# Block 0 of a recurrence with a feed-forward layer: one written order of instructions and loads for all sixteen steps

## The chip, the cores and the metric

The kernel runs on one core of one Trainium2 chip. A core has five engines with a queue of instructions each: PE (TensorE, matmuls), DVE (VectorE), ACT (ScalarE), POOL (GpSimd) and SP (SyncE, which issues the loads here). Each works through its own queue in order and waits at semaphores for the others. The metric is the device time of one execution in microseconds (us), as the median of several runs.

## The reference, cut to what matters

```python
# r, k, v: [B=4, H=8, S=768, D=48], w, u: [H, D], all float32
state = zeros(B, H, D, D)
for t in range(S):
    cur = (u * k[t]) outer v[t]
    y[t] = r[t] @ (state + cur)
    state = w * state + k[t] outer v[t]
x = y as [B * S = 3072, H * D = 384]
h = x @ w_in                          # w_in: [384, 2048]
g = where(h > 0, h, exp(min(h, 0)) - 1)
out = g @ w_out                       # w_out: [2048, 384]
```

## The kernel before, in words

The 768 positions are cut into 6 chunks of 128. A unit (n, b) is one batch b in chunk n, and a block is the four units of a chunk, 512 token columns. In a unit r and k are turned by PE (`turn_in`, L628), scaled by powers of w (`decay_r`, `decay_k`, through `scaled`, L688), multiplied to scores inside the chunk (`scores`, L768), masked or taken over by copies (`mask_scores` at the start, `take_scores`, L849, later), and multiplied by v; the state of the chunk before is added (`by_state`, `by_keys`, `added_state`). A token's own term, r times u times k, is made by `key_product` and `times_u` (L724, L728), summed by `current_sum` (L733) and either put on the scores' diagonal (`diag_scores`, L838 on ACT, L842 on POOL) or, in block 0, multiplied by v (`current_by_v`, L859). `key_rest` (L740) multiplies k by the power of w that is left to the end of the chunk, which the new state needs. `split_x` (L949; `split_turned`, L899 and L901, in block 0) gives the outputs as a high and a low part.

The feed-forward layer of a block goes in 16 steps f of 128 hidden columns: `hidden` (L1031: nine matmuls, since x and the weights stand as high and low parts), `negative` (L1040 and L1041 on ACT: relu and exp), `elu` (L1046 on DVE), `split_g` (L1052 the high part on ACT, L1054 the low one on DVE) and `project` (L1083, nine matmuls that gather in PSUM). The hidden steps have two buffers in PSUM, so step f needs the buffer that the low part of an earlier g gave back.

The weights are loaded within block 0, in stages of one w_out and one w_in slice: `load_weights(j)` is w_in of step j/2 for even j (four DMAs, L212), w_out for odd j (L215). Three stages are held at a time. Pair k (w_out of step k-1, w_in of step k) is brought to its high and low parts by `widen` (ACT, L571), `merge` (DVE, L580), `split_w` (w_out's on POOL, L591; w_in's on ACT, L593) and `rest_w` (w_out's on POOL, L615, or DVE; w_in's on DVE, L617).

The order on every engine follows from the order in which the program calls these functions. Before, three strings set it for block 0: START (written out, to the first half of hidden step 0), BOTH (written out, steps 0 to 2) and FIRST, a pattern that `step` goes through once for each of the steps 3 to 15 and in which an entry with a digit or x means "the unit that is at this stage now" (a unit of block 1 begins at the steps of BEGIN). LATER is the pattern of blocks 1 to 5. The short names are the keys of the tables of operations: `wd`, `ma`, `sp`, `rs` (or `rsd`, on DVE) for the weights, `T`, `dr`, `dk`, `A`, `ru`, `sum`, `kr` (`krd` on DVE) for a unit, `Lw:j` for a load of weights, `Lrk`, `Lv`, `Lnk`, `Lnv`, `rk`, `v` for loads of r and k or v.

Of the kernel before, what the change touches and what calls it, by code (L numbers as in the profile page):

```python
# [8 lines left out]
F32 = mybir.dt.float32  # L9
# [10 lines left out]
P = 128  # L20
# [7 lines left out]
T = B * P  # L28
# [8 lines left out]
EARLY = (0, 6)  # L37
# [22 lines left out]
BEGIN = [2, 5, 8, 11]  # L60
# [6 lines left out]
class Kernel:  # L67
# [232 lines left out]
    def run(self):  # L300
        self.start()
        self.first_steps()
        for at in range(3, NCH * NF):
            self.step(*divmod(at, NF))
        for f in (NF - 2, NF - 1):
            self.project(NCH - 1, f)
        self.store(NCH - 1)

    def start(self):
# [3 lines left out]
        for b in (2, 3):  # L313
# [33 lines left out]
            "m1a": lambda b: self.mask_scores(0, b, 1, True),  # L347
            "vd": lambda b: self.current_by_v(0, b),
# [34 lines left out]
    def first_steps(self):  # L383
# [44 lines left out]
    def step(self, n, f):  # L428
        nc = self.nc

        k = f + 2 if n == 0 else NF + 1
        units = self.stages(n, f)


        last = divmod(n * NF + f - (1 if (n, f) < EARLY else 2), NF)
        both = {
            "ru": lambda n, b: self.current(n, b),
            "kr": lambda n, b: self.key_rest(n, b),
            "A": lambda n, b: self.scores(n, b),
            "sw": lambda n, b: self.decay_state(n, b),  # L440
# [725 lines left out]
```

## Time and profile before

| | |
|---|---|
| median of 3 runs | 497.28 us (496.21 to 499.79) |
| profiled execution, its own time | 496.31 us |
| its span in the profile | 494.6 us |
| mean granted clock of PE | 0.999 |
| PE matmul | 485.3 us busy, 98% of the span |
| PE weight loads (beside the matmuls) | 403.4 us, 82% |
| DVE | 304.2 us, 61% |
| ACT | 240.7 us, 49% |
| POOL | 107.3 us, 22% |

Busy times are sums over the whole span, so a share is a mean over stages that differ. The profile also cuts the span in 40 slices of 12.4 us and gives the busy share of each in tenths; its lines of PE and DVE are

```profile
PE   8999999999999999999999999999999999999995
DVE  7899988884686557657556575574674343433332
```

Block 0 is the first nine slices.

### The profile page before, as it was taken

What the parts mean: (1) busy time and instruction counts of PE and PEld (TensorE: products, weight loads), DVE (VectorE), ACT (ScalarE), POOL (GpSimd) and SP (SyncE); (2) the same over time, 40 slices, a digit from 0 to 9 for tenths busy, and PEclk for the clock granted to TensorE, in tenths of its full rate; (3) what the DMA queues carried; (4) which work ended last, traced back from release to release, by engine and by line L of the source; (5) the groups of instructions that cost most, each with busy time, mean ns of one, the idle gap of its engine ahead of it and who ended that gap; (6) DMA issues with size and microseconds to landing.
All of it is one profiled execution on the core that took longest, in us unless ns stands there. A gap on an engine that the chain in (4) does not pass through costs nothing.

```text
span 494.6 us, 12125 instructions
## 1 busy us (share of the span) xinstructions
PE 485.3 (98%) x5013; PEld 403.4 (82%) x5013; DVE 304.2 (61%) x533; ACT 240.7 (49%) x458; POOL 107.3 (22%) x142
## 2 busy tenths in 40 slices
PE   8999999999999999999999999999999999999995
PEld 7787778787888888888888888888888888889995
DVE  7899988884686557657556575574674343433332
ACT  4377766734454444535435435445354453344341
POOL 7623332441132331221321321301011000000000
PEclk9999999999999999999999999999999999999999
DMA  9899987483364652544513625514343000010001
GB/s 142 223 231 204 213 197 190 94 153 89 84 139 105 135 121 43 130 118 72 121 52 84 151 67 108 142 44 92 101 79 100 11 1 2 8 33 20 5 0 69
DMA packets 108453, 49.11 MB, mean 99 GB/s; under 512 B 89442, under 2 KB 104292, under 8 KB 108388
## 3 DMA queue, kind: packets, MB, share of 16 engines
q1 hardware_dynamic: 96292, 43.52, 40.0%
q10 hardware_dynamic: 12096, 4.72, 4.0%
q8 instruction: 41, 0.67, 0.6%
q14 instruction: 24, 0.20, 0.1%
HBM read 35.12 MB, written 13.11 MB: 98 GB/s over the span
## 4 chain that ended last, share of the span: by engine, by line
PE 93%; DMA 3%; SPq 2%; DVE 1%; issue 0%; ACT 0%; DVEq 0%
PE ps_acc L1083 40%; PE ps_h L1031 39%; PE ps_y L824 4%; PE ps_a L792 4%; PE ps_y L812 1%; PE ps_y L924 1%; PE ps_a L768 1%; PE ps_y L807 1%; DMA raw<-in_k_dram 1%; DMA stage<-in_moe_w_out_dram 1%; DMA r_t<-in_r_dram 1%; SPq L169 1%; PE ps_y L880 1%; SPq L165 1%; PE ps_kT L628 0%; DMA w_col<-in_w_dram 0%
## 5 line engine op out<-in xcount | busy, mean ns | idle before, releaser
L1031 PE MATMUL ps_h<-x,wh 128*128 128x512 f32 (+1 forms) x582 | 192.6, 388 | 0.0
L1083 PE MATMUL ps_acc<-g,wh 128*128 128x512 f32 x480 | 164.6, 397 | 0.1
L1046 DVE SCALAR_TENSOR_TENSOR ps_h<-g,ps_h 128x512 f32<-128x512 f32 x96 | 66.6, 694 | 123.8 <-ACT g L1041 123.6
L1031 PEld LDWEIGHTS ps_h<-x,wh 128*128 128x128 f32 x582 | 108.8, 188 | 23.0 <-DVE g L1054 0.5
L1040 ACT ACTIVATE g<-ps_h 128x512 f32<-128x512 f32 x96 | 57.3, 596 | 123.2 <-PE ps_h L1031 95.0
L1031 PE MATMUL ps_h<-x,wl 128*128 128x512 f32 (+1 forms) x291 | 112.7, 387 | 0.0
L1083 PEld LDWEIGHTS ps_acc<-g,wh 128*128 128x128 f32 x480 | 90.0, 188 | 21.2 <-issue 0.8
L1054 DVE SCALAR_TENSOR_TENSOR g<-ps_h,g 128x512 fp32r<-128x512 f32 x96 | 66.3, 690 | 45.3 <-ACT g L1052 40.4
L1083 PE MATMUL ps_acc<-g,wl 128*128 128x512 f32 x240 | 93.6, 390 | 0.0
L1052 ACT ACTIVATE g<-ps_h 128x512 fp32r<-128x512 f32 x96 | 57.4, 598 | 72.7 <-DVE ps_h L1046 62.7
L1031 PEld LDWEIGHTS ps_h<-x,wl 128*128 128x128 f32 x291 | 54.7, 188 | 10.9
L1041 ACT ACTIVATE g<-g 128x512 f32<-128x512 f32 x96 | 60.7, 632 | 3.1
L842 POOL TENSOR_TENSOR a<-ident,diag 128x512 f32<-128x512 f32 x20 | 20.9, 1044 | 149.9 <-PE ps_y L924 81.2
L1083 PEld LDWEIGHTS ps_acc<-g,wl 128*128 128x128 f32 x240 | 45.1, 188 | 8.5
L676 POOL TENSOR_TENSOR tb<-rk,qw 128x512 f32<-128x512 f32 x16 | 20.7, 1297 | 70.3 <-DMA rk<-blocks 61.2
L1083 PE MATMUL ps_acc<-wh,g 128*128 128x384 f32 x128 | 33.8, 335 | 0.0
L849 DVE COPY_PREDICATED a<-mask,ps_a 128x512 f32<-128x512 int32 x40 | 29.3, 732 | 0.0
L838 ACT ACTIVATE a<-ident,diag 128x128 f32<-128x128 f32 x80 | 25.3, 391 | 0.0
L1083 PEld LDWEIGHTS ps_acc<-wh,g 128*128 128x128 f32 x128 | 23.2, 188 | 0.3
L571 ACT ACTIVATE wide<-stage 128x768 f16<-128x768 bf16 (+1 forms) x18 | 17.8, 991 | 9.9 <-DMA stage<-in_moe_w_in_dram 8.7
L949 ACT CAST x<-ps_y 128x256 fp32r<-128x256 f32 (+1 forms) x40 | 10.8, 324 | 22.8 <-DVE state L939 21.4
L1083 PE MATMUL ps_acc<-wl,g 128*128 128x384 f32 x64 | 21.4, 335 | 0.0
(114 smaller groups left out, 440.2 us busy)
## 6 DMA issues: line engine op xcount, KB each, us to landing
blocks<-tb SPq DMA_DIRECT2D x64, 128.0 KB, 2.3
rk<-blocks SPq DMA_DIRECT2D x16, 512.0 KB, 3.4
stage<-in_moe_w_out_dram SPq DMA_DIRECT2D x16, 383.8 KB, 5.4
stage<-in_moe_w_in_dram SPq DMA_DIRECT2D x64, 95.8 KB, 4.3
out_dram<-stage ACTq DMA_DIRECT2D x80, 48.0 KB, 1.7
r_t<-in_r_dram SPq DMA_DIRECT2D x17, 192.0 KB, 4.3
k_t<-in_k_dram SPq DMA_DIRECT2D x17, 192.0 KB, 4.9
v_t<-in_v_dram SPq DMA_DIRECT2D x17, 192.0 KB, 5.3
```

The source lines that it names most:

```text
L676: (self.nc.gpsimd if i else self.nc.vector).tensor_mul(dst, src, by)
L792: nc.tensor.matmul(un["pa"][i][keys, a * P : (a + 1) * P], lhsT=un["k"][rows, a, keys], rhs=un["r"][rows, a, :], start=True, stop=True, sk ...
L838: self.nc.scalar.activation(un["a"][i][:, a, :], self.ident, AF.Copy, scale=diag[:, a : a + 1])
L842: self.nc.gpsimd.tensor_mul(un["a"][i], self.ident.unsqueeze(1).to_broadcast([P, HP, P]), diag.unsqueeze(2).to_broadcast([P, HP, P]),)
L849: self.nc.vector.copy_predicated(un["a"][i], self.mask.bitcast(I32).unsqueeze(1).to_broadcast([P, HP, P]), un["pa"][i].rearrange("p (a t) ...
L1031: self.nc.tensor.matmul(ph[:, part], lhsT=a[:, c * P : (c + 1) * P], rhs=x[:, c, part], start=(c == 0 and i == 0), stop=(c == NC - 1 and i ...
L1040: nc.scalar.activation(g, ph, AF.Relu, scale=-1.0)
L1041: nc.scalar.activation(g, g, AF.Exp, scale=-1.0)
L1046: self.nc.vector.scalar_tensor_tensor(ph, g, -1.0, ph, op0=ALU.add, op1=ALU.max)
L1052: nc.scalar.activation(part, g, AF.Copy, scale=W_SCALE)
L1054: nc.vector.scalar_tensor_tensor(part, g, W_SCALE, self.g[n, f][2].bitcast(F32), op0=ALU.mult, op1=ALU.subtract)
L1083: self.nc.tensor.matmul(at, lhsT=lhs, rhs=rhs, start=(f == 0 and i == 0), stop=(f == NF - 1 and i == 2),)
```

## The change

BOTH, `BEGIN`, `EARLY` and `now` are gone. START ends with the first half of hidden step 0 as before; FIRST now holds each instruction and each load of the rest of block 0 once, with the step or pair that it is for. `name@n.b` is an operation of the unit (n, b). `first_steps` goes through that string, and `run` calls `step` from the first step of block 1 on. The operations of a unit come from one table, `unit_ops`. Among the entries, the eight key rests that were `krd` are `kr` (POOL), four `rud` are `ru` (POOL), two `swd` (the state's decay) are `sw` (POOL), and two weight rests that were `r3` (POOL) are `rsd`. Two of START's masks are `m0a` and `m1a` (ACT's copy, then POOL), one of which was so before; three `vd` are `vdd` (DVE). `d0` and `d1` stand in the table but in no string.

```diff
-START = """
-Lrk:2 Lv:1 Lrk:3 Lv:2 Lw:0 Lv:3 Lw:2 Lw:1 Lw:4 Lw:3 Lw:5
...
+START = """
+jk:8 Tr:0 inv pr ub rua:0 Lrk:2 Tk:0 zw Tr:1 PT rub:0 dr:0 dk:0 Tk:1 A:0 dr:1 dk:1 Lrk:3 sum:0 m0:0 kr:0 vdd:0 A:1
...
+Y:0 sum:3 m1:2 vdd:1 sum:2 A:3 m0a:2 xh:0 vdd:2 wd:0 Lw:2 m1:3 ma:0 m0:3 Y:1 vd:3 kr:2 xh:1 xl:0 sp:0 kr:3 Lw:3 Y:2
+rsd:0 wdi:1 xl:1 mai:1 xh:2 wdo:1 Y:3 xl:2 xh:3 spi:1 Lw:4 kr:1 xl:3 H:0 Lnk:0 mao:1 Lw:6 Sd:3 wd:2
-BOTH = """
-xh:3 xl:2 xl:3 hid0 rsd:2 krd:2 wd:2 neg0 krd:1 spo:1 hid1 ma:2 elu0 sp:2 gh0 rs:1 Lnk:0 rs:3 neg1 Lw:8 gl0 Sd:1 rsd:4
...
 FIRST = """
-Lq rk3 v3 Eq1 hid ns3 A1 T0 rud0 ma sum0 bkA-1 neg df0 elu sp dk0 pa1 brA-1 Y2 gh gl dr0 pb1 r4d xh2 xl2 mbT+1 mrT+1
-proj krd1 swd2 Dp0 r3 rudx rudA-2 sumA-1 wd third tT+0
+hid0 spo:1 neg0 Lw:5 rsd:2 ma:2 Sd:1 rs:1 Lw:7 sp:2 S:2 elu0 gh0 Lw:8 hid1 rs:3 rsd:4 wd:3 Lw:9 neg1 T@1.0 hid2 gl0
+dk@1.0 ma:3 Lw:10 ru@1.0 sp:3 proj0 elu1 sum@1.0 gh1 neg2 gl1 Dq@1.0 proj1 rsd:6 Lnk:1 wd:4 dr@1.0 Lw:12 ma:4 Lnv:0
+rs:5 wd:5 hid3 kr@1.0 sp:4 elu2 Dp@1.0 ma:5 gh2 rsd:8 sp:5 gl2 rs:7 Lw:11 A@1.0 Lw:14 neg3 rsd:10 elu3 ru@1.1 swd@1.0
...
-        for at in range(3, NCH * NF):
+        for at in range(NF, NCH * NF):
...
-        for op in BOTH.split():
-            if ":" in op:
+        units = self.unit_ops()
+        for op in FIRST.split():
+            if op == "third":
+                self.third_slot()
+            elif "@" in op:
+                name, at = op.split("@")
+                n, b = (int(i) for i in at.split("."))
+                self.done.add((name, n, b))
+                units[name](n, b)
+            elif ":" in op:
                 self.do(op)
             else:
-                layer[op[:-1]](int(op[-1]))
+                name = op.rstrip("0123456789")
+                layer[name](int(op[len(name):]))
...
-        for op in (LATER if n else FIRST).split():
+        for op in LATER.split():
...
     def mask_scores(self, n, b, i, by_act=False):
         un = self.units[n, b]
-        t = self.wk.tile([P, T], F32, tag=f"g_{i}", name="a", bufs=3)
-        a = un.setdefault("a", {})[i] = t.rearrange("p (a t) -> p a t", a=HP)
+        if i in un.setdefault("a", {}):
+            self.take_scores(n, b, i)
+            return
+        a = self.place_scores(n, b, i)
```

On SP, the queue of loads behind the first ones (w_in and w_out are the feed-forward weights, the four `32x3x511` rows of one w_in slice are shown as one). Before:

```order
L169 DMA v_t1_73<-in_v_dram 128x8x48
L165 DMA raw_185<-in_r_dram 128x8x48
L165 DMA raw_185<-in_k_dram 128x8x48
L169 DMA raw_185<-in_v_dram 128x8x48
L212 DMA stage_181<-in_moe_w_in_dram 32x3x511 x4
L169 DMA raw_185<-in_v_dram 128x8x48
L212 DMA stage_181<-in_moe_w_in_dram 32x3x511 x4
L215 DMA stage_181<-in_moe_w_out_dram 128x1535
```

and after:

```order
L171 DMA raw_185<-in_r_dram 128x8x48
L171 DMA raw_185<-in_k_dram 128x8x48
L175 DMA v_t1_73<-in_v_dram 128x8x48
L218 DMA stage_181<-in_moe_w_in_dram 32x3x511 x4
L175 DMA raw_185<-in_v_dram 128x8x48 x2
L221 DMA stage_181<-in_moe_w_out_dram 128x1535
L218 DMA stage_181<-in_moe_w_in_dram 32x3x511 x4
L221 DMA stage_181<-in_moe_w_out_dram 128x1535
```

The r and k of batch 3 moved ahead of v of batch 1, and the second slice of w_in behind the first of w_out.

On ACT, from the widening of pair 2 on, around the first two steps of the layer. Before:

```order
L571 ACTIVATE wide_182<-stage_181 128x768
L1040 ACTIVATE g_561<-ps_h_536 128x512
L1041 ACTIVATE g_561<-g_561 128x512
L593 ACTIVATE wh2_128<-stage_181 128x384
L1052 ACTIVATE g_0_580<-ps_h_536 128x512
L1040 ACTIVATE g_586<-ps_h_566 128x512
L1041 ACTIVATE g_586<-g_586 128x512
L571 ACTIVATE wide_182<-stage_181 128x768
```

and after:

```order
L554 ACTIVATE wide_182<-stage_181 128x768
L1038 ACTIVATE g_583<-ps_h_536 128x512
L1039 ACTIVATE g_583<-g_583 128x512
L576 ACTIVATE wh2_128<-stage_181 128x384
L939 COPY state2_61<-ps_st_612 48x4x48 x2
L1050 ACTIVATE g_0_632<-ps_h_536 128x512
L554 ACTIVATE wide_182<-stage_181 128x768
L1038 ACTIVATE g_652<-ps_h_638 128x512
L1039 ACTIVATE g_652<-g_652 128x512
```

The widening of pair 3 moved from behind relu and exp of step 1 to ahead of them.

On POOL, from the last products with v of block 0 on to the first weight parts (L859 is `current_by_v`, L591 and L615 the parts of w_out). Before:

```order
L859 TENSOR_TENSOR vd_407<-raw_185,diag_373 128x384
L686 TENSOR_TENSOR a_419<-a_419,mask_111 128x512
L859 TENSOR_TENSOR vd_460<-raw_185,diag_422 128x384
L591 CAST wh1_126<-stage_181 128x384
L591 CAST wh2_128<-stage_181 128x384
L615 TENSOR_TENSOR wl1_127<-stage_181,wh1_126 128x384
L615 TENSOR_TENSOR wl2_129<-stage_181,wh2_128 128x384
```

and after:

```order
L669 TENSOR_TENSOR a_409<-a_409,mask_111 128x512
L846 TENSOR_TENSOR vd_455<-raw_185,diag_391 128x384
L723 TENSOR_TENSOR raw_185<-raw_185,rev_58 128x8x48 x2
L723 TENSOR_TENSOR k_t1_72<-k_t1_72,rev_58 128x8x48
L574 CAST wh1_126<-stage_181 128x384
L598 TENSOR_TENSOR wl1_127<-stage_181,wh1_126 128x384
L574 CAST wh2_128<-stage_181 128x384
L598 TENSOR_TENSOR wl2_129<-stage_181,wh2_128 128x384
L707 TENSOR_TENSOR ru_684<-r_t0_68,k_t0_69 128x384
L711 TENSOR_TENSOR ru_684<-ru_684,u_b_87 128x384
```

Three key rests (L723) and the product of r, k and u of the first unit of block 1 (L707, L711) came in from DVE.

## Rows read from the trace of the kernel before

**Rows 1.** Windows: start and end, us, busy PE PEld DVE ACT POOL, clock, DMA, GB/s.

```profile
25.00:107.17 82.17, 81.26 (x826) 65.72 (x825) 73.32 (x133) 56.83 (x104) 28.68 (x38) 1.00 0.87 187
140.00:490.00 350.00, 349.31 (x3473) 292.71 (x3471) 190.40 (x324) 158.92 (x309) 52.94 (x58) 1.00 0.32 72
```

**Rows 2.** Chain that ended last, in order of time: start us, us, what.

```profile
10.41 4.74 DMA raw<-in_k_dram
25.02 4.42 PE ps_h L1031 x27
...
35.81 2.06 PE ps_acc L1083 x9
41.00 2.27 PE ps_acc L1083 x9
47.26 2.28 PE ps_acc L1083 x9
...
62.65 2.26 PE ps_acc L1083 x9
...
107.17 2.04 PE ps_h L1031 x9
```

**Rows 3.** Timeline of PE: start us, us, operation, idle before in brackets.

```profile
45.24 0.45 PE L807 MATMUL ps_y<-rk,state 48*32 48x128 f32 x16
...
59.99 0.45 PE L807 MATMUL ps_y<-rk,state 48*32 48x128 f32 x16
...
72.61 1.16 PE L768 MATMUL ps_a<-rk 48*128 48x128 f32 x16 [0.65 <-DVE rk L688]
```

**Rows 4.** Timeline of DVE.

```profile
19.79 1.29 DVE L688 TENSOR_TENSOR a<-ps_a,mask 128x512 f32<-128x512 f32 x2 [1.02 <-PE ps_a L768]
21.00 1.20 DVE L580 SCALAR_TENSOR_TENSOR stage<-stage,wide 128x384 int32<-128x384 int32 x1
...
25.19 1.01 DVE L901 TENSOR_TENSOR x<-ps_y,x 128x384 fp32r<-128x384 f32 x2
...
32.77 0.70 DVE L1046 SCALAR_TENSOR_TENSOR ps_h<-g,ps_h 128x512 f32<-128x512 f32 x1
...
34.37 0.68 DVE L1054 SCALAR_TENSOR_TENSOR g<-ps_h,g 128x512 fp32r<-128x512 f32 x1
...
104.35 1.19 DVE L724 TENSOR_TENSOR ru<-r_t,k_t 128x384 f32<-128x384 f32 x1
```

**Rows 5.** Durations by line over the span: min/median/max ns, first and last start.

```profile
L740 POOL TENSOR_TENSOR k_t<-k_t,rev x8: 1017/1024/1032, 110.1 to 314.0; 128x384 f32<-128x384 f32 x8
L740 DVE TENSOR_TENSOR k_t<-k_t,rev x6: 547/550/749, 9.8 to 94.0; 128x384 f32<-128x384 f32 x6
...
L580 DVE SCALAR_TENSOR_TENSOR stage<-stage,wide x18: 546/950/1198, 21.0 to 101.1; 128x768 int32<-128x768 int32 x14, 128x384 int32<-128x384 int32 x4
```

**Rows 6.** Timeline of ACT.

```profile
21.44 0.66 ACT L571 ACTIVATE wide<-stage 128x384 f16<-128x384 bf16 x1 [0.63 <-DMA stage<-in_moe_w_in_dram]
...
30.56 0.63 ACT L1041 ACTIVATE g<-g 128x512 f32<-128x512 f32 x1
31.10 1.07 ACT L571 ACTIVATE wide<-stage 128x768 f16<-128x768 bf16 x1
```

**Rows 7.** DMA issues on SP (start us, us), and median us from issue to landing.

```profile
25.77 0.77 SPq L165 DMA_DIRECT2D k_t<-in_k_dram  x1
...
32.05 2.23 SPq L212 DMA_DIRECT2D stage<-in_moe_w_in_dram  x4
...
stage<-in_moe_w_out_dram SPq DMA_DIRECT2D x16, 383.8 KB, 5.4
...
stage<-in_moe_w_in_dram SPq DMA_DIRECT2D x64, 95.8 KB, 4.3
```

**Rows 8.** Timeline of POOL.

```profile
20.50 1.28 POOL L686 TENSOR_TENSOR a<-a,mask 128x512 f32<-128x512 f32 x1 [1.52 <-ACT a L685]
...
103.83 1.29 POOL L676 TENSOR_TENSOR tb<-rk,qw 128x512 f32<-128x512 f32 x1
```

More of the change, by code (lines that the diff above doesn't have):

```diff
@@ L55 @@
+gl12 mb@2.0 neg13 pb@1.3 pa@1.3 ma:16 Y@1.3 proj12 sp:16 rsd:30 hid15 rs:27 elu13 neg14 ru@2.0 gh13 rsd:31 xh@1.3
+mr@2.0 gl13 sw@1.3 elu14 gh14 sum@2.0 xl@1.3 rs:29 neg15 br@2.0 elu15 bk@2.0 gh15 v@1.3 ns@1.3 proj13 gl14 third
+rk@1.3 v@1.2 proj10 gl15
 """
@@ L426, in third_slot, with unit_ops @@
         self.load_v(2, 1)
-    def step(self, n, f):
+    def unit_ops(self):
         nc = self.nc
[L431 to L436, printed above, removed]
+        return {
             "ru": lambda n, b: self.current(n, b),
@@ L470, in step @@
         }
+    def step(self, n, f):
+        last = divmod(n * NF + f - 2, NF)
+        units = self.unit_ops()
         layer = {
-            "hid": lambda: self.hidden(n, f, self.rest_of(n, f)),
-            "ma": lambda: self.merge(k),
+            "hid": lambda: self.hidden(n, f),
             "neg": lambda: self.negative(n, f),
-            "sp": lambda: self.split_w(k),
-            "r4": lambda: self.rest_w(k, 1),
-            "r3": lambda: self.rest_w(k, 0),
-            "r4d": lambda: self.rest_w(k, 1, nc.vector),
-            "r3d": lambda: self.rest_w(k, 0, nc.vector),
             "elu": lambda: self.elu(n, f),
@@ L495, in step @@
                 continue
-            if op[-2] in "+-":
-                name, times = op[:-3], {"A": SCORES, "Y": OUTPUTS, "T": TURNS}[op[-3]]
-                for m, b in self.units_at(times, now - int(op[-2:])):
-                    if (name, m, b) not in self.done:
-                        self.done.add((name, m, b))
-                        {**both, **moved}[name](m, b)
-                continue
-            name, stage = op[:-1], -1 if op[-1] == "x" else int(op[-1])
-            for at, m, b in units:
-                todo = {**both, **by_pe}
-                if at == stage and name in todo and (name, m, b) not in self.done:
+            name, times = op[:-3], {"A": SCORES, "Y": OUTPUTS, "T": TURNS}[op[-3]]
+            for m, b in self.units_at(times, now - int(op[-2:])):
+                if (name, m, b) not in self.done:
                     self.done.add((name, m, b))
-                    todo[name](m, b)
+                    units[name](m, b)
     def warm(self, times):
@@ L780, in insertion, with inserted @@
             return
-        nc, un = self.nc, self.units[new[0]]
+        self.inserted(new[0], old[0] if old else None)
+    def inserted(self, new, old):
+        nc, un = self.nc, self.units[new]
         un["pa"] = [self.bank("a") for _ in range(2)]
-        was = self.units[old[0]] if old else None
+        was = self.units[old] if old else None
         if was:
@@ L797, in insertion @@
             return
[L798 to L800 removed]
+        self.by_state(*old)
+        self.by_keys(*old)
+        self.added_state(*old)
     def by_state(self, n, b):
@@ L821, in by_keys @@
             y, t = (un["py"][0], j * P) if len(un["py"]) == 1 else (un["py"][j // 2], j % 2 * P)
+            begins = n == 0 and (j != 1 if len(un["py"]) > 1 else j == 0 and "vd" not in un)
             for a in range(HP):
@@ L825, in by_keys @@
                     y[self.pair(a), t : t + P], lhsT=v[:, d : d + Q], rhs=un["a"][i][:, a, :],
-                    start=(n == 0 and j != 1 and len(un["py"]) > 1), stop=bool(last), skip_group_check=True,
+                    start=begins, stop=bool(last), skip_group_check=True,
                 )
@@ L875, in first_outputs @@
         py = self.bank("y")
-        vd = un["vd"].rearrange("p h d -> p (h d)")
-        for c in range(NC):
+        for c in range(NC if "vd" in un else 0):
+            vd = un["vd"].rearrange("p h d -> p (h d)")
             for a in range(HP):
```

60 lines of the change are left out of this document (26 added, 34 removed).

## The prediction

> **What bounds the kernel now.** I read the profile in four steps: the busy time by window, the chain of waits, PE's own waits up to 120 us, and then the timelines of DVE, ACT, POOL and SP over block 0, which is the only place the change touches.
>
> The windows come first. From 25.00 to 107.17 us, which is the feed-forward part of block 0, PE is busy for 81.3 of 82.17 us at a granted clock of 1.00, DVE for 73.3, ACT for 56.8 and POOL for 28.7 [rows 1]. From 140 to 490, PE is busy for 349.31 of 350. So PE sets the end everywhere, and nothing in the later blocks can move: the LATER string and its table are the same. In the chain, each group of nine matmuls costs 2.04 us, or 2.27 with the change of kind before it, in block 0 as later. Hidden step 0 starts at 25.02, and step 16, the first of block 1, at 107.17 [rows 2]. The order of after issues the same matmuls between those points (16 hidden steps, 14 projections, four units of scores and outputs). **What can be gained is therefore the idle time of PE before 107.17, and only that**; any new wait of PE there is lost whole, since nothing later has slack to take it up.
>
> Inside block 0 two places are loose [rows 3]. At 72.61 the scores wait 0.65 us for DVE (the scaled r and k). The outputs that start at 59.99 take until 62.65, or 2.66 us, where those from 45.24 to 47.26 take 2.02: there k decayed to the end of the chunk, a DVE operation, came late. Together 1.29 us. Ahead of 25.02 PE is fed by DVE, whose longest wait there is 1.02 us for scores, at 19.79: that goes back, by the chain, to the load of k of batch 3, issued at 10.41 and landed 4.74 later [rows 2, 4].
>
> **The change part by part.** *Start.* SP now issues r and k of batches 2 and 3 together, ahead of v1, so k of batch 3 lands earlier by the issue of one such load, about 1 us (a k took 0.77 [rows 7]), and most of the 1.02 us is gained on DVE. Up to the low half of x of batch 1, DVE loses two key rests, one merge and one mask and gains three products with v: with some 0.5 for each operation of this width [rows 5] that is -3 x 0.5 - 0.65 + 3 x 0.5 = -0.65. The merge at 21.00, which took 1.20 [rows 4], would take 0.55: another -0.65 if nothing new collides. So the first half of hidden step 0 could start up to 2.3 us earlier. The second half cannot, since it needs the high and low parts of x of batch 3; the low ones of batches 2 and 3 ended at 25.19 + 1.01 = 26.20 before. ACT makes the high parts, and now stands in order behind the widening of w_in1 and w_out0. w_in1 was there at 21.44 [rows 6] and is now issued behind w_out0, a load of 384 KB; with r and k of batch 3 ahead of everything, v1 and w_in0 move too. I put its delay at 1.5 us, an estimate between nothing and the 2.23 that the four issues of a slice take [rows 7], so widening begins at about 23, two widenings (0.66 each) and two high parts (0.5 each, as the low ones in [rows 4]) end at 25.3, the low part follows by 0.5: 25.8. The end of hidden step 0 gains **0.4** (bounds: a loss of 0.6 and a gain of 2.3).
>
> *Step 1's negative part behind a widening.* On ACT, the widening of pair 3 (w_out2, w_in3) now stands ahead of step 1's relu and exp; before, it stood behind them, and they ended at 30.56 + 0.63 = 31.19 [rows 6]. In SP's queue w_out2 is moved past block 1's first r and k and w_in3: the issue of that k ended at 25.77 + 0.77 = 26.54, so w_out2 goes out then, and lands 5.4 us later, at 31.9 [rows 7]. Widening (1.07) and relu and exp (twice 0.63) then end at 34.2, 3.0 late. Of this DVE takes up 1.58, because it began the ELU of step 1 only at 32.77, and PE 0.76, because the low part of g was ready at 34.37 + 0.68 = 35.05 and projection 1 began at 35.81 [rows 2, 4]. That leaves 0.66, plus the 0.4 by which PE comes earlier; if the load takes less, nothing. Bounds 0 and 1.1; I take **+0.75**, nearer the median landing.
>
> *Hidden step 4.* Its PSUM buffer is that of step 2, freed by the low part of g2, whose high part stands on ACT behind the widening of pair 5, which waits for w_in5. If that goes out as before, it lands at 34.28 + 4.3 = 38.6 [rows 7]. Then 1.07 of widening, 0.5 for a weight split, 0.63 (a pass of ACT over 128x512) and 0.68 for the two parts of g2: 41.5 [rows 4, 6]. PE stood at this point (four hidden steps, two projections, one unit's scores done) at 41.00 [rows 2]; with the two terms above at 41.35. So **+0.15** (0 to 1).
>
> *DVE to POOL.* Eight key rests go from DVE (0.55 each) to POOL (1.02), and four products of r, k and u likewise (two operations each of the same shape; the last is the one at 104.35 [rows 4]): 16 operations, 16.3 us more on POOL, 8.8 less on DVE. In return DVE takes two weight rests from POOL (0.55 each there, about 1.0 on POOL) [rows 5]; four small halves of state decay, which go to POOL too, I leave out. Two of the key rests lay ahead of 25 us. So from 25 to 107 DVE falls from 73.3 by 14 x 0.55 - 1.1 to 66.7 of 82.2, and POOL rises from 28.7 to about 43. With that the two loose places of before close: **-1.3** (bounds -1.3 and 0). The cover of POOL's slower operations is their lead: a key rest is needed only at the outputs, a step or more later.
>
> *Other new order.* From step 5 to 15, operations change places in every step, and projections and hidden steps are no longer in turn (hidden 8 ahead of 7, projection 5 behind 9, projection 10 last). With two PSUM buffers for the hidden steps, each hidden step waits for the low part of the one two before it in the written order. Counting the DVE queue in front of those, I find hidden 7 and 8 and one turn of k within 0.4 us of being late; I take **+0.65** of PE waits in all (bounds 0 and 3).
>
> *Shared access of DVE and POOL.* In the trace an operation of DVE with two inputs in SBUF is stretched when POOL works on SBUF: the merge at 21.00 took 1.20, not 0.55, beside POOL's mask from 20.50 to 21.78, and the product at 104.35 took 1.19 beside POOL's 1.29 us from 103.83 [rows 4, 5, 8]. So one such meeting costs about 0.65. With POOL busy half of the time, not a third, and DVE's share of such operations down by 14, I count some 4 to 6 more meetings. DVE has room for 3 to 4 us, and what reaches PE is between 0 and 2.5; I take **+0.5**. The Trainium skill ("SBUF — State Buffer", the section on who interferes with whom) states for this an exclusive lock between DVE and GpSimd, with the second blocked whole; the two stretched rows agree. By that rule alone, taken for every meeting, the moved work would have been better left on DVE, and the sum would be that of the second rival.
>
> Sum: -0.4 + 0.75 + 0.15 - 1.3 + 0.65 + 0.5 = +0.35. The profiled execution took 496.31 us (span 494.6), so 496.31 + 0.35 = **496.7**. The median of the three runs shown, 497.28, is 0.97 above that execution; the highest is 499.79. The profiled execution is therefore a low one of its kind, and a median of after may stand above the sum by as much.
>
> **The rivals.** *The start's gain is kept and no new wait comes.* PE would start 1 to 2 us earlier and lose both old waits: -1.3 with -0.4 to -2.3, that is 492.7 to 494.6; likeliest 494.2. For it: PE's dense run from 25 leaves each engine but DVE with room [rows 1]. Against it: ACT's queue at the start, whose loads set the second half of step 0.
>
> *The lock decides (slower).* Place: DVE from step 3 on. If each of the about 30 merges and weight rests of DVE, with POOL busy for half of the time, met an operation of POOL, 15 meetings of 0.65 are 9.8 us. DVE has 82.2 - 66.7 = 15.5 us of slack on the whole, but its queue is in order, and behind each stands an ELU or a low part of g that PE waits for. With a third reaching PE, +3.3 in place of +0.5: 496.7 + 2.8 = 499.5, and up to 503 with two thirds. The deciding point is where a low part of g ends later than PE arrives, which is within 0.4 us at three places. Against it: of the six key rests on DVE before, five took 0.55 and one 0.75 [rows 5]. By the rule of the Trainium skill named above this would be the likely case.
>
> *One long wait of order.* A load or a widening that stands far ahead in its queue holds an engine for several steps; price over 5 us, above 502. Nothing in the order that I followed shows it.
>
> *The change does little* (the orders differ, and PE is covered either way) gives 496.3, inside the forecast.
>
> **How the numbers follow.** Forecast, the sum with its own bounds (495 to 499): 0.55. Start's gain kept: 0.22. Lock: 0.18. Long wait: 0.05. The range reaches down into the second case and up into the third, 493.6 to 500.4, and leaves out about 0.1 on each side. A measurement of this kernel tells about 1% (5 us) from no change. Faster by over that would need 492.3 or less, more than the whole loose time before 107.17: 0.02. Slower, 502.3 or more, needs the lock at its worst or the long wait: 0.08. Within: 0.90.
>
> **What would show it.** In the profile of the changed kernel: hidden step 0 ends within 0.5 us of its time before; PE's waits list shows no wait for scaled r and k at the second unit, and new ones at projection 1 and hidden 4; step 16 starts between 106 and 110; DVE busy near 67 and POOL near 43 us from 25 to 107; DVE's merges and rests have maxima above 1.1 us more often than before. I am wrong if step 16 starts before 105.5 (no new waits), or if PE idles more than 3 us between steps 3 and 16, and it shows then whether a stretched DVE operation or a load was the last thing waited for.

## The result, and the profile after

The changed kernel takes 501.54 us (median of 10 runs, 499.77 to 503.04), the kernel before 496.97 (495.73 to 499.79): the ratio is 1.0081, with a 95% interval of 1.0062 to 1.0100. By the ratio it is 4.0 us slower (4.6 by the medians). The forecast was 496.7, the range ended at 500.4.

The windows of the profile after, in the columns of [rows 1], START's first:

```profile
0.00:25.00 25.00, 21.29 (x374) 18.23 (x378) 20.44 (x43) 9.09 (x16) 21.01 (x39) 1.00 0.88 176
25.00:107.17 82.17, 78.47 (x826) 63.03 (x815) 73.66 (x115) 53.95 (x97) 46.87 (x51) 1.00 0.78 183
140.00:490.00 350.00, 349.35 (x3470) 292.42 (x3469) 192.76 (x326) 160.61 (x313) 55.10 (x60) 1.00 0.33 73
```

From 25 to 107 us PE is busy for 78.5 us, not 81.3; the later blocks are as full as before. Since PE is further back at 107.17 than before, the other engines are compared up to the start of step 16, at equal work:

```profile
25.00:110.88 85.88, 82.18 (x842) 66.12 (x831) 76.36 (x121) 55.44 (x99) 50.58 (x57) 1.00 0.79 183
```

DVE has 12 operations less there (121, not 133 [rows 1]) and is busy 3.0 us longer (76.36, not 73.32). POOL went from 28.7 to 50.6. The chain names the start of hidden step 16:

```profile
110.88 2.04 PE ps_h L1029 x9
```

Before, that was 107.17 [rows 2]: 3.71 us of the 4.6 by which the profiled spans differ (499.2 and 494.6) are lost ahead of it. The list of PE's own waits up to 130 us (what waited, for what; total, times, longest), without the wait for the first constants:

```profile
PE ps_h L1029 <- DVE g L1052: 2.7, 3, 1.5
...
PE ps_y L878 <- issue: 1.2, 1, 1.2
PE ps_st L922 <- issue: 0.9, 1, 0.9
PE ps_y L878 <- DVE vd L846: 0.4, 1, 0.4
```

and where the large ones stand in PE's timeline:

```profile
24.18 0.31 PE L878 MATMUL ps_y<-ident,vd 128*32 128x128 f32 x3 [1.20 <-issue]
...
29.91 0.46 PE L922 MATMUL ps_st<-raw 128*32 128x48 f32 x24 [0.88 <-issue]
...
44.30 0.50 PE L1029 MATMUL ps_h<-x,wh 128*128 128x512 f32 x1 [1.48 <-DVE g L1052]
...
66.75 0.50 PE L1029 MATMUL ps_h<-x,wh 128*128 128x512 f32 x1 [1.00 <-DVE g L1052]
```

The first two lie in and behind START, with a releaser that the profile doesn't show ("issue"); the last two are hidden steps 4 and 7 (a third, of 0.19, is step 8, which the expectations below call 6), which wait for a low part of g, that is, for a PSUM buffer. Where PE starts hidden step 0, and where it is done with hidden steps 0 and 1 and three states, after and then before:

```profile
25.40 0.39 PE L1029 MATMUL ps_h<-x,wh 128*128 128x256 f32 x1
...
32.48 0.60 PE L611 MATMUL ps_rT<-ident,r_t 128*128 128x128 f32 x4
```

```profile
24.95 0.39 PE L1031 MATMUL ps_h<-x,wh 128*128 128x256 f32 x1
...
30.56 0.50 PE L1083 MATMUL ps_acc<-g,wh 128*128 128x512 f32 x1
```

Measured at equal work of PE, the account is: 0.45 late at the first half of hidden step 0 (25.40, before 24.95), about 2.0 when hidden steps 0 and 1 and the three states are done (32.5, before 30.6), 3.4 at the first unit's outputs (they end at 50.67, before 47.26), 3.7 at step 16. The two old waits of [rows 3] are gone, as forecast.

What DVE did ahead of hidden step 4, and POOL and ACT at the same time:

```profile
39.02 1.84 DVE L563 SCALAR_TENSOR_TENSOR stage<-stage,wide 128x768 int32<-128x768 int32 x1 [0.27 <-ACT wide L554]
...
41.38 0.95 DVE L563 SCALAR_TENSOR_TENSOR stage<-stage,wide 128x768 int32<-128x768 int32 x1
42.26 1.39 DVE L600 SCALAR_TENSOR_TENSOR wl<-stage,wh 128x384 fp32r<-128x384 f32 x1
43.57 0.68 DVE L1052 SCALAR_TENSOR_TENSOR g<-ps_h,g 128x512 fp32r<-128x512 f32 x1
```

```profile
39.01 1.04 POOL L723 TENSOR_TENSOR k_t<-k_t,rev 128x384 f32<-128x384 f32 x1
...
41.42 1.81 POOL L829 TENSOR_TENSOR a<-ident,diag 128x512 f32<-128x512 f32 x1
```

```profile
41.50 0.60 ACT L1050 ACTIVATE g<-ps_h 128x512 fp32r<-128x512 f32 x1
```

The low part of g2 ended at 44.25, and step 4 started at 44.30. Ahead of it on DVE stood two merges and a weight rest; one merge took 1.84 and not 0.95, beside a key rest on POOL, and the rest 1.39 and not 0.55, beside scores on POOL. The high part of g2 was done on ACT at 42.10: straight behind it, the low part would have ended at 42.78, and PE was ready at 42.82. So it is DVE's queue that makes the wait. Over the kernel the weight rests of w_in, all between 536 and 559 ns before, and those of w_out on DVE (min/median/max ns) are now:

```profile
L600 DVE SCALAR_TENSOR_TENSOR wl<-stage,wh x16: 517/580/1387, 22.6 to 100.1; 128x384 fp32r<-128x384 f32 x16
...
L598 DVE TENSOR_TENSOR wl<-stage,wh x4: 787/1166/1370, 59.3 to 101.2; 128x384 fp32r<-128x384 f32 x4
```

On ACT, the widenings that stand ahead of layer work wait for their loads:

```profile
24.11 0.66 ACT L554 ACTIVATE wide<-stage 128x384 f16<-128x384 bf16 x1 [1.88 <-DMA stage<-in_moe_w_in_dram]
...
33.23 1.09 ACT L554 ACTIVATE wide<-stage 128x768 f16<-128x768 bf16 x1 [1.04 <-DMA stage<-in_moe_w_out_dram]
34.19 0.56 ACT L1038 ACTIVATE g<-ps_h 128x512 f32<-128x512 f32 x1
...
62.34 1.09 ACT L554 ACTIVATE wide<-stage 128x768 f16<-128x768 bf16 x1 [3.28 <-DMA stage<-in_moe_w_in_dram]
63.30 0.57 ACT L1038 ACTIVATE g<-ps_h 128x512 f32<-128x512 f32 x1
```

w_in1 is widened at 24.11 (before 21.44 [rows 6]), step 1's relu starts at 34.19, and step 8's at 63.30, behind a widening of pair 9; from there g8 and with it hidden step 7 are late.

### The profile page after: what moved, and what is told of

Read it like the earlier page. It is cut to its first block, busy times and chain, and to the rows that moved or that the text cites. A ratio compares the mean times of both kernels' runs of the same rounds, so it can differ in the third digit from the quotient of the medians.

```text
span 499.2 us, 12130 instructions
## 1 busy us (share of the span) xinstructions
PE 485.4 (97%) x5013; PEld 403.3 (81%) x5013; DVE 306.4 (61%) x517; ACT 238.2 (48%) x451; POOL 130.9 (26%) x160
## 4 chain that ended last, share of the span: by engine, by line
PE 83%; DMA 3%; SPq 3%; ACT 3%; DVE 3%; POOL 2%; issue 1%; ACTq 0%; DVEq 0%; POOLq 0%
PE ps_acc L1081 37%; PE ps_h L1029 35%; PE ps_a L778 4%; PE ps_y L811 3%; SPq L218 2%; DMA stage<-in_moe_w_in_dram 2%; DMA stage<-in_moe_w_out_dram 1%; PE ps_y L798 1%; ACT wide L554 1%; PE ps_y L922 1%; PE ps_y L793 1%; POOL wl L598 1%; SPq L171 1%; DVE ps_h L1044 1%; ACT g L1050 1%
## 5 line engine op out<-in xcount | busy, mean ns | idle before, releaser
L1081 PE MATMUL ps_acc<-g,wh 128*128 128x512 f32 x480 | 162.9, 395 | 0.6 <-issue 0.5
L829 POOL TENSOR_TENSOR a<-ident,diag 128x512 f32<-128x512 f32 x22 | 24.6, 1121 | 155.4 <-PE ps_y L922 88.8
L825 ACT ACTIVATE a<-ident,diag 128x128 f32<-128x128 f32 x72 | 22.8, 390 | 0.0
```

The source lines that it names most:

```text
L825: self.nc.scalar.activation(un["a"][i][:, a, :], self.ident, AF.Copy, scale=diag[:, a : a + 1])
L829: self.nc.gpsimd.tensor_mul(un["a"][i], self.ident.unsqueeze(1).to_broadcast([P, HP, P]), diag.unsqueeze(2).to_broadcast([P, HP, P]),)
L1081: self.nc.tensor.matmul(at, lhsT=lhs, rhs=rhs, start=(f == 0 and i == 0), stop=(f == NF - 1 and i == 2),)
```

## The experiments

Ratios are to the kernel before, run alongside, with 95% intervals. One hundredth is 5 us. The edits are shown cut to the entries that change.

**Halves, and the work that was moved.** Four kernels: the change with all moved operations back on DVE (`kr` to `krd`, `ru` to `rud`, `sw` to `swd`); the same for blocks 1 and 2 alone; before's START with the written rest; the new START with before's rest. The last two change START as a whole, besides these lines:

```diff
 # old_start: before's START, and the written rest begins
-hid0 spo:1 neg0 Lw:5 rsd:2 ma:2 Sd:1 rs:1 Lw:7 sp:2 S:2 elu0 ...
+xh:3 xl:2 xl:3 hid0 krd:2 wd:2 neg0 krd:1 spo:1 rsd:2 ma:2 Sd:1 rs:1 Lnk:0 Lw:7 sp:2 S:2 Sd:3 elu0 ...
 # old_rest: the new START, and before's BOTH without what START has done
-xh:3 xl:2 xl:3 hid0 rsd:2 krd:2 wd:2 neg0 krd:1 spo:1 ...
+hid0 rsd:2 Lw:5 neg0 spo:1 ...
```

> The written order with all key rests, the four products of r, k and u and the two halves of state decay back on DVE (order untouched). Theory POOL (the work that was moved to POOL stretches DVE's operations, and POOL's own queue gives the weight stages back late): the three waits of hidden steps for a low part of g, 2.7 us, go mostly, so about 499 against 501.5 for the whole change and 497.0 before. Theory ORDER (the new order of loads, widenings and steps costs the time): 501.5 or more, since DVE gets about 9 us of work back. DVE's weight rests go back to a median of 0.55 and a maximum under 0.8 by POOL; by ORDER the rows of DVE change but step 16 starts no earlier than 110.5.

> As the kernel with all back on DVE, but only for the units of blocks 1 and 2; block 0's own key rests stay on POOL. Theory POOL: the waits of the hidden steps 4, 6 and 7 go as there, about 498.5 to 499. Theory START (most of the loss lies ahead of hidden step 2, in the order of the first loads and instructions): 500 to 501.5, about 2 us of loss left before hidden step 2.

> Before's START (its order of loads and instructions, key rests of block 0 on DVE), then the written order of the change from hidden step 0 on. Theory START: hidden 2 comes about 1.8 us earlier, 499.5 or less. Theory POOL or ORDER in the rest: the waits of hidden 4, 6 and 7 stay, and the gain is 0.5 to 1.8 us at most, 499.7 to 501.

> The START of the change, then before's order (its three written steps and its repeated pattern, with the moved operations on DVE). Theory START: about 1.8 us slower than before, 498.8. Theory POOL or ORDER in the rest: near before plus what the start costs now, 497 to 498.8; if it is below 497 the start's gain of up to 1 us was real and only the rest lost it.

| | median us | ratio |
|---|---|---|
| all_on_dve | 505.85 | 1.0188 (1.0158 to 1.0218) |
| first_on_dve | 505.58 | 1.0192 (1.0154 to 1.0230) |
| old_start | 498.90 | 1.0046 (1.0020 to 1.0071) |
| old_rest | 498.53 | 1.0033 (1.0006 to 1.0061) |

The first two fell against theory POOL: with the work back on DVE the same order loses another 4 us by the medians, 5 by the ratios. In this order the move to POOL helps more than it costs. The stretched operations are real, and they do not go with the move back. Count, from hidden step 0 to step 16, the operations of DVE on SBUF alone that took over 0.2 us longer than their kind's median before: in the kernel before it is one, by 0.64 us; in the change 15, by 8.5 us together; in all_on_dve still 10, by 5.5, and in first_on_dve 11, by 6.4; in old_start 14, by 6.6, and in old_rest one, by 0.95. All of them stand beside an operation of POOL. The halves add up: 1.6 us for START and 2.3 for the rest, each give or take 1.3, 3.9 together, against 4.0 for the whole change.

**The moved work in before's order.** on_pool moves the same operations to POOL and touches no order. rest_on_pool leaves block 0's own key rests on DVE:

```diff
-            "nru": lambda b: self.now("rud", b, self.current, dve),
+            "nru": lambda b: self.now("rud", b, self.current),
...
-proj krd1 swd2 Dp0 r3 rudx rudA-2 sumA-1 wd third tT+0
+proj kr1 swd2 Dp0 r3 rudx ruA-2 sumA-1 wd third tT+0
...
-            "rud": lambda n, b: self.current(n, b, nc.vector),
+            "rud": lambda n, b: self.current(n, b, nc.vector if n > 1 or b == 3 else None),
-            "swd": lambda n, b: self.decay_state(n, b, nc.vector),
+            "swd": lambda n, b: self.decay_state(n, b, None if (n, b) in ((1, 1), (1, 3)) else nc.vector),
```

> The kernel before, its order untouched, with the same operations moved to POOL as in the change: the eight key rests, the four products of r, k and u and two halves of state decay. Theory POOL (the moved work stretches DVE and delays POOL's weight parts): slower than before, by 1.5 to 3 us, 498.5 to 500, with DVE's merges and rests stretched as in the change. Theory ORDER (moving helps, and the order of loads, widenings and steps costs the time): 496 to 497, and the one wait of the scores for scaled r and k (0.65) goes.

> The kernel before, with only block 1's and 2's operations moved to POOL (four key rests, four products, two halves of state decay); block 0's own key rests stay on DVE, since on POOL they made the first hidden step wait 0.95 us. Theory COVER (in before's order the moved work is hidden on POOL and closes the 0.65 us wait of the scores): 495.5 to 496.7, 0.3 to 1 us below before. Theory LOCK (DVE stretched by POOL takes it back): 496.7 to 497.7.

on_pool: 497.37 us, 1.0015 (1.0000 to 1.0029), a little above what theory ORDER gave and well below theory POOL: the whole move, in before's order, gains nothing. rest_on_pool: 496.40, **0.9975 (0.9959 to 0.9991)**, faster than both kernels by a little, as theory COVER had it, though a wait of 0.4 us of the scores stays. Its windows row, and PE's waits behind START's first constants:

```profile
25.00:107.17 82.17, 81.54 (x824) 65.94 (x825) 70.31 (x118) 56.80 (x104) 43.20 (x54) 1.00 0.89 192
```

```profile
PE ps_h L1031 <- DVE x L901: 0.6, 1, 0.6
PE ps_a L768 <- DVE rk L688: 0.5, 2, 0.4
PE ps_y L924 <- issue: 0.5, 1, 0.5
```

15 operations fewer on DVE bring 3.0 us less, not some 7: about half is eaten by stretching (by the count above, six operations and 3.8 us). No low part of g is late. Where the gain of 1.2 us comes from the profile does not show: PE is busy there for 81.54 us, before 81.26, and this execution's span, 495.5, is not below before's 494.6.

**The stop inside START.** The "issue" of 1.20 us stands in the middle of a group of products that has a wait only at its first one. In all kernels with the new START up to here it stood behind the same 19th product. no_junk takes eight turns of the identity out of PE's program at the start (`jk:8` to `jk:0`), 16 recorded instructions:

> The change without the eight turns of the identity that keep PE busy at the start (16 fewer of PE's recorded instructions ahead). Theory FETCH (the gap of 1.2 to 2.3 us in the last outputs of block 0 is a fetch of instructions): it moves by 8 matmuls to a later place in the program, behind the products of the 19th, and keeps above 0.8 us; the time is 500.5 to 502.5. Theory WAIT (something unrecorded is waited for there): it stays behind the 19th product.

502.17 us, 1.0117 (1.0086 to 1.0148). The stop moved by eight matmuls, as theory FETCH asks, and is 0.70 long, a little less than it gave:

```profile
24.73 0.60 PE L878 MATMUL ps_y<-ident,vd 128*32 128x128 f32 x13
25.12 0.38 PE L811 MATMUL ps_y<-a,raw 128*32 128x128 f32 x3
26.21 0.64 PE L811 MATMUL ps_y<-a,raw 128*32 128x128 f32 x16 [0.70 <-issue]
```

Counted in PE's records (matmuls, weight loads and some 80 others), it stands within one of number 705 in every kernel that has it. The change's other stops with "issue" in the middle of a group, and those of before and of the experiments up to 190 us, stand within one of 961, 3009 and 4289, which is 705 plus 1, 9 and 14 times 256. The page counts 41 packets on its instruction queue, of 16 KB each, one for 256 instructions of PE. The packet list of the trace gives their times; record 449 is one block of 256 ahead of 705:

| START's instructions, first loads | passes record 449 | fetch | stop at 705 |
|---|---|---|---|
| old, old (before) | 19.71 | 21.16 to 22.41 | 0.2 |
| old, new (new_loads) | 19.17 | 20.67 to 21.95 | 0.4 |
| new, old (start_instructions) | 19.91 | 22.38 to 23.55 | 1.30 |
| new, new (the change) | 19.12 | 21.61 to 22.60 | 1.20 |
| new, new (old_rest) | 20.20 | 23.08 to 24.67 | 1.85 |

PE goes on 1.2 to 1.6 us after the end of the fetch wherever it had to stop, at 705 and at the later places: it is so in all 43 stops over 0.15 us of the 20 traces. In the twelve kernels with START's new order of instructions the stop at 705 is 0.4 to 2.3 us, in the eight with the old order at most 0.4. One execution does not give its size: seven kernels are the same up to hidden step 0 (the change and, of the experiments here and below, first_on_dve, late_wide, rk_early, x_first, rests_on_pool and no_split), and their stops are 0.43 to 1.91 us. In all seven, the time from record 449 to hidden step 0 is 5.1 us plus the stop: the stop comes on top whole.

**Loads or instructions of START.** new_loads is the kernel before with the first loads in the change's order; start_instructions has the new START with the old loads, and before's rest; old_loads is the whole change with the old loads. Of new_loads' edit the start is shown; in BOTH, `Lnk:0` and `Lw:7` move ahead with it.

```diff
 # new_loads
-Lrk:2 Lv:1 Lrk:3 Lv:2 Lw:0 Lv:3 Lw:2 Lw:1 Lw:4 Lw:3 Lw:5
+Lrk:2 Lrk:3 Lv:1 Lw:0 Lv:3 Lv:2 Lw:1 Lw:2 Lw:3 Lw:4
...
-rsd:0 mai:1 Lw:6 krd:3
+rsd:0 mai:1 Lnk:0 Lw:6 Lw:5 krd:3
```

> The change with the order of the first loads as before (up to w_in4), all instructions of the engines in the change's order. Theory LOADS (the new order of loads holds PE's fetch of instructions back for 1.2 us inside the last outputs of block 0, at the same instruction in all four kernels with that START, and makes w_in1 late): the gap there falls to 0.3 or less and hidden step 2 comes 1 to 2 us earlier, 499.5 to 500.5. Theory PACE (the fetch is late because PE reaches its place sooner after asking for it, whatever is loaded): the gap stays above 0.8, 501 to 502.

> The kernel before with nothing but the order of its first loads as in the change (up to w_in4). Theory LOADS: PE's fetch of instructions starts over 2.4 us after PE passes the instruction that asks for it (1.45 before), and PE stops 1 us or more in the last outputs of block 0; with w_in1 late as well, 498 to 499. Theory PACE (the fetch is late because PE passes the stretch faster): stop of 0.5 or less, 496.5 to 497.7.

> The START of the change in its order of instructions, but with the first loads in before's order, and before's rest. Theory LOADS: the gap in the last outputs is 0.5 or less, and the time 496 to 497.5. Theory PACE: the gap stays over 1 us, 498 to 499.

old_loads: 502.60 us, 1.0122 (1.0092 to 1.0153). new_loads: 499.41, 1.0042 (1.0019 to 1.0064). start_instructions: 498.37, 1.0030 (1.0005 to 1.0055). As for the stop, LOADS fell: with the new loads alone there is none of 1 us, with the new instructions alone it is 1.30. old_loads, with a stop of 0.54, falls between the two theories, and its time above both: PE waits there for loads of k instead, 1.4 and 1.3 us. But the new loads cost 2.1 us by themselves, in another way. The lines are PE's and ACT's in new_loads:

```profile
25.65 0.39 PE L1031 MATMUL ps_h<-x,wh 128*128 128x256 f32 x1 [0.98 <-ACT x L899]
...
26.81 0.50 PE L1031 MATMUL ps_h<-x,wh 128*128 128x256 f32 x2 [0.65 <-DVE x L901]
```

```profile
23.71 0.66 ACT L571 ACTIVATE wide<-stage 128x384 f16<-128x384 bf16 x1 [3.45 <-DMA stage<-in_moe_w_in_dram]
```

w_in1 comes 2.3 us later than before, ACT waits for it with the high parts of x queued behind, and both halves of hidden step 0 wait. In the whole change these waits don't show: PE stands at its fetch in the same microseconds. New loads alone cost 2.1 us, new instructions alone 1.5, both together 1.6 (old_rest). The interval of each is about 2.5 us wide, so that the sizes are no finer than that.

**The rest of block 0.** late_wide puts the widenings and merges of pairs 3, 5 and 9 behind the layer work that they stood ahead of; rk_early adds the loads of r and k of two units directly behind the outputs that free their place; x_first puts, with late_wide, the low parts of x of two units ahead of weight rests. no_split makes the state of batch 3 behind hidden step 0 and not between its halves; rests_on_pool puts `rsd:13`, `17`, `21` and `31` back on POOL.

```diff
 # late_wide
-wd:3 Lw:9 neg1 T@1.0
+neg1 Lw:9 wd:3 T@1.0
-Lw:12 ma:4 Lnv:0 rs:5 wd:5 hid3 kr@1.0 sp:4 elu2 Dp@1.0 ma:5 gh2 rsd:8 sp:5 gl2 rs:7
+Lw:12 elu2 ma:4 Lnv:0 rs:5 gh2 gl2 wd:5 hid3 kr@1.0 sp:4 Dp@1.0 ma:5 rsd:8 sp:5 rs:7
-ns@1.0 wd:9 neg8 pa@1.1
+ns@1.0 neg8 wd:9 pa@1.1
-Lw:19 ma:9 sp:9 elu8 gh8 hid7 gl8
+Lw:19 elu8 gh8 gl8 ma:9 sp:9 hid7
 # x_first, besides
-hid7 ru@1.2 rsd:18 T@1.2 rsd:17 xh@1.1 gl6
+hid7 ru@1.2 T@1.2 xh@1.1 gl6 xl@1.1 rsd:18 rsd:17
-Y@1.2 rsd:24 rud@1.3
+Y@1.2 xh@1.2 rsd:24 xl@1.2 rud@1.3
 # no_split
-xl:3 H:0 Lnk:0 mao:1 Lw:6 Sd:3 wd:2
+xl:3 H:0 Lnk:0 mao:1 Lw:6 wd:2
-neg0 Lw:5 rsd:2 ma:2 Sd:1
+neg0 Lw:5 rsd:2 ma:2 Sd:3 Sd:1
```

> The change with pairs 3, 5 and 9 widened and merged behind relu and exp of step 1, both parts of g2, and the whole of g8, instead of ahead of them. Theory WIDEN (these stand on ACT and DVE behind a widening that waits for its load): the waits of hidden 4 (1.48) and hidden 7 (1.00) go, 499 to 499.5. Theory POOL (DVE stretched by POOL makes the low parts late wherever they stand): half of it or less, 500.3 to 501.5.

> The kernel with the late widenings, and the loads of r and k of the units 2 and 3 of block 1 put in SP's queue directly behind the outputs that free their place, ahead of the weight loads that wait for a stage. Theory QUEUE (in the change these loads stand on SP behind weight loads that wait for DVE's weight rests, and the third unit's turn waits 1.4 to 2.5 us for its k as soon as PE comes earlier): that wait goes, and with it what the late widenings should have given: 499 to 500. Theory NOISE (the order as a whole has no slack, another wait takes its place): 501 or more.

> Before's START with the written rest of the change, late widenings and early loads of r and k. If the costs of START (1.5 us) and of the rest (1.9) are separate, and QUEUE holds: 496 to 497.5, about the kernel before. If another wait takes their place: 498.5 to 500.

> The change with the state of batch 3 made behind hidden step 0 instead of between its two halves. Two changes of kind less on PE, by the difference of the groups' times (6.14 against 5.61 us for the same work) up to 0.5 us: 500.5 to 501.5, hidden step 1 at most 0.5 earlier. If the second half waits for x of batch 3 anyway, no change.

> The change with the late widenings, and with the low parts of x of the units 1 and 2 of block 1 ahead of the weight rests and of the product that stood before them on DVE. Theory QUEUE ON DVE (what PE waits for in the rest of block 0 stands on DVE behind weight work that waits for a load or is stretched beside POOL; the turn of a unit needs the bank that the low part of x of the unit before frees): the waits of hidden 4 and 7 and of the turns of units 2 and 3 (2.5 and 0.5 in the kernel with late widenings) go, 499 to 500; the gap of the fetch stays. Theory NO SLACK (another wait appears): 501 or more.

> The same with before's START. QUEUE ON DVE: 496 to 498. NO SLACK: 499 or more.

> The change with the four rests of w_out that it put on DVE (0.79 to 1.37 us each, stretched beside POOL) back on POOL. Theory DVE LOAD (in this order every delay on DVE reaches PE: 6.6 us more on DVE cost 4 us): a gain of 1 to 2 us, 499.5 to 500.7. Theory STAGES (POOL gives the weight stages back later, so loads come later): no gain or a loss, 501 to 503.

| | median us | ratio |
|---|---|---|
| late_wide | 504.17 | 1.0154 (1.0098 to 1.0209) |
| rk_early | 505.96 | 1.0175 (1.0149 to 1.0200) |
| old_start_rk_early | 505.42 | 1.0149 (1.0118 to 1.0180) |
| no_split | 501.22 | 1.0078 (1.0053 to 1.0103) |
| x_first | 503.45 | 1.0112 (1.0080 to 1.0144) |
| old_start_x_first | 501.36 | 1.0080 (1.0053 to 1.0107) |
| rests_on_pool | 501.22 | 1.0110 (1.0068 to 1.0152) |

None of them gains beyond its interval, and rk_early and old_start_rk_early lose beyond it, against the change and old_start. The expectations of late_wide, rk_early and old_start_rk_early missed: the times lie above the figures of both theories. x_first and old_start_x_first came out as NO SLACK, rests_on_pool as STAGES. late_wide took hidden 4's wait from 1.48 to 0.55 and hidden 7's away, and lost 2.5 us at the turn of k of unit 2. I had put that on the load of k; rk_early, in which that k was in SBUF long before, shows the same stop. It is the low part of x of the unit before, which frees the bank. PE and DVE in rk_early:

```profile
71.46 0.63 PE L611 MATMUL ps_kT<-ident,k_t 128*128 128x128 f32 x4 [2.50 <-issue]
```

```profile
67.61 1.36 DVE L600 SCALAR_TENSOR_TENSOR wl<-stage,wh 128x384 fp32r<-128x384 f32 x1 [0.62 <-ACT wh L576]
68.89 1.34 DVE L598 TENSOR_TENSOR wl<-stage,wh 128x384 fp32r<-128x384 f32 x1
70.15 0.68 DVE L1052 SCALAR_TENSOR_TENSOR g<-ps_h,g 128x512 fp32r<-128x512 f32 x1
70.75 0.60 DVE L949 TENSOR_TENSOR x<-ps_y,x 128x256 fp32r<-128x256 f32 x2
```

The low part of x ends at 71.35, behind two stretched weight rests that waited for ACT. In late_wide such a stop cost more than its length, since PE's clock fell with it:

```profile
72.04 1.09 PE L611 MATMUL ps_kT<-ident,k_t 128*128 128x128 f32 x4 [2.49 <-issue]
...
73.36 0.63 PE L1029 MATMUL ps_h<-x,wl 128*128 128x512 f32 x1
...
75.58 0.40 PE L1029 MATMUL ps_h<-x,wl 128*128 128x512 f32 x1
```

From 71.75 to 75.16 us the granted clock is 0.50 (1.2 and not 2.4 GHz), afterwards 1.00 again. PE is busy for 3.12 of these 3.41 us at half its speed, so that some 1.6 us are lost (an estimate). The profiled executions of old_loads (from 45.83, behind the 1.64 us wait of hidden step 4), old_start_rk_early (from 61.76, behind one of 2.35) and new_loads (from 27.27, behind its two waits) have such a stretch too; those of rk_early, with a stop of 2.50, and of the change have none in block 0. So the spans of these four say less about their order than they seem to. x_first moved the low part of x ahead of the weight rests; that stop went, and hidden steps and scores wait 0.5 to 1.0 us at five places:

```profile
PE ps_h L1029 <- DVE g L1052: 2.4, 3, 1.0
...
PE ps_h L1029 <- DVE wl L600: 0.6, 1, 0.6
PE ps_a L751 <- DVE rk L671: 0.5, 1, 0.5
```

In rests_on_pool hidden 4 still waits 1.18 us. There the change had put four rests of w_out on DVE and taken two others off it. no_split neither gains nor loses: theory "up to 0.5" can't be told from nothing here.

**The faster version, and the one load.** rest_on_pool_k_early is rest_on_pool with `Lrk:2 Lrk:3 Lv:1` in place of `Lrk:2 Lv:1 Lrk:3`.

> The faster version (before's order, block 1's and 2's operations on POOL), with r and k of batch 3 loaded ahead of v of batch 1 as in the change, all other loads as before. If the wait of 1.0 us for that k sets when the first hidden step begins: 495.4 to 496.2. If x and w_in1 set it: 496.2 to 497.

496.33 us, 0.9983 (0.9970 to 0.9996), no better than rest_on_pool. PE no longer waits for k, and waits 1.25 us at hidden step 0 for ACT's high part of x. So in this order the wait for k that the change removed was not what set the start.

## Why the prediction was wrong

- **Start** (forecast -0.4): the step that failed, by the largest miss. START alone costs 1.6 us (old_rest). PE's fetch of instructions stood at nothing in the sum, since before shows 0.2 us of it at most; in the change it stops PE for 1.20 us ahead of hidden step 0, where a stop comes on top whole, and for 0.88 behind it. The wait for k of batch 3 did go, from 1.04 to 0.16. The delay of w_in1, put at 1.5 us, was 2.7 in this execution (24.11, not 21.44) and 0.9 to 1.7 in the six other kernels with this START; the low part of x of batch 3 ended at 26.59 and not 25.8. PE waited for neither here, though by itself that order of loads costs 2.1 us. Some 0.6 of the 2.0 us lost up to 32.48 lie in hidden steps 0 and 1 and three states, which take 6.2 us without the stop and took 5.6 before; no_split brings them to 5.9 in its trace, and no run explains the other 0.3.
- **Step 1's negative part** (+0.75): relu started at 34.19, 4.3 us late, as the chain of load, widening and relu said. But PE was itself 2 us late by then and did not wait: nothing.
- **Hidden step 4** (+0.15, at most 1): right place, half of the chain, size wrong, 1.48. The sum followed ACT's queue to the high part of g2. The merge and the weight rest that stand on DVE ahead of the low part were not in it, nor their stretching; the high part was done in time.
- **DVE to POOL** (-1.3): both old waits went. DVE's busy time did not fall to 67 but was 73.7 in the same window, and 76.4 at equal work.
- **Other new order** (+0.65, at most 3): hidden 8 and 7 and one turn of k wait 0.19, 1.00 and 0.15, so 1.3. All three had been named, at 0.65 together.
- **Shared access** (+0.5): a meeting was priced at 0.65; the two in the rows above took 0.8 to 0.9. Expected were 4 to 6 more; there were 14 more, 15 in all with 8.5 us. Two of them, 1.7 us together, stand ahead of the low part that hidden 4 waited for. The exclusive lock of the Trainium skill ("SBUF — State Buffer", "Who interferes with whom") agrees with them. The prediction's use of it as a rule against the move fails: the move back costs 4 to 5 us here, and in before's order the move gains 1.2 us for blocks 1 and 2 alone (rest_on_pool) and nothing as a whole (on_pool).

Of the 3.7 us at step 16, these terms make 2.0 + 0 + 1.5 - 1.3 + 1.3 = 3.5; what shared access costs is inside them.

So the time fell where the second rival had put it, 499.5 to 503, and its 15 meetings were there. What it concluded, that the moved work was better left on DVE, is refuted. Whether the meetings make the rest's loss is not: they come with the written rest (old_start 14, old_rest one), on whichever engine the moved work stands (10 and 11 with it on DVE), and no run kept the order and took them away. About 1.6 us are START's and 2.3 the rest's. For the rest, what is shown is that its order reacts to more work on DVE (some 15 operations, about 4 us of busy time up to step 16, cost 4 to 5) where before's order takes it up (16 operations make 1.2), and that most waits are of one kind: an operation of DVE that frees a PSUM bank stands behind weight work that waits for a load or is stretched. Which part of the order causes that stays open; seven kernels did not find one part whose return gives the time back. Open is too why the fetch is late with the new instructions of START: it begins 0.2 to 3.4 us behind record 449 in the 20 traces, and the stretch from record 449 to 704 takes 3.59 us in the change and 3.80 before, which explains 0.2 of a stop of 1.2.

A last 0.9 us of the spans' difference lies behind step 16; 0.48 of it is a stop at record 4290, again one of the fetch.

## What to carry to other kernels

When a step is moved in a kernel that keeps its main engine full, the loads are as much part of the order as the instructions: ask of each load what stands behind its first use on the engine that waits for it. Cost moved work at the lengths that it will have beside its new neighbours, not at the median of before. An order written by hand is best measured in halves, which here put the loss in both, and a single idea in it (here a part of the work moved to POOL) may be worth more alone.

## What the runs showed of the hardware that was not expected

PE stopped at some of the places 256 recorded instructions apart for 0.2 to 2.3 us, in the middle of a group, until 1.2 to 1.6 us after a 16 KB packet of its instruction queue had landed. The profile shows it as a wait for "issue"; that it stands at the same count of records in every kernel, and moves when instructions are taken out ahead, tells it from a wait. The Trainium skill ("Runtime: NRT & Kernel Launch", "Instruction fetch mechanics") says that instructions come in blocks of 16 KiB, 256 of them, and that the cost at a block's edge is mostly hidden. The size agrees. That the cost is mostly hidden agrees too, with three stops at some 39 edges in the change; two of the three lie around its first hidden step, where they took 2.1 us. Up to 25 us DMA is busy for 0.88 of the time. Whether that is why was not settled, since before's 0.2 us stand beside a share of 0.90.

A wait of PE can cost more than it lasts: in four of the twenty profiled executions the granted clock was 0.50 for 3.4 us at the end of or behind a wait of PE in block 0, and a matmul of 512 columns then came every 0.42 us and not every 0.23. Other waits as long left it at 1.00.
